# Laying the inputs of an attention, Fourier-mixing and feed-forward kernel out on the host

## The chip, the cores and the metric

The kernel runs on one core of a Trainium2 chip. The metric is the device time of one execution in microseconds. What the host does with the inputs before the launch, and with the output after it, is not part of that time.

## The reference

Eight batches of 576 tokens go through an attention of 8 heads of 64 channels, a Fourier mixing and a feed-forward layer. The attention has two parts that are added: a local one, in which a token sees the 7 tokens nearest to it, and a pooled one over means of 4 tokens.

```python
q_d = q.reshape(B, H, Sd, factor, D).mean(axis=3)           # factor 4, also k_d and v_d
out_d = sm_attn(q_d, k_d, v_d)
out_up = np.repeat(out_d, factor, axis=2)
mask = np.abs(pos[:, None] - pos[None, :]) < factor
scores = np.where(mask, scale * np.matmul(q, k.transpose(0, 1, 3, 2)), -1000000000.0)
x = out_up + softmax(scores) @ v                            # then (B, S, H * D)

mixed = np.real(np.fft.fft(np.fft.fft(x, axis=1), axis=2))
u = x + mixed
un = (u - mean(u)) / np.sqrt(var(u) + 1e-06)
out = u + np.maximum(un @ w_ch1, 0.0) @ w_ch2               # 512 -> 2048 -> 512
```

q, k and v are float32, the two weight matrices float64.

## The kernel before

**Phase 1** (the loop `while s < STEPS`, L836) makes the attention and the Fourier mixing. The local attention is cut into 40 units, five to a batch; a unit is a pair of windows of 64 tokens within a span of 128 tokens (`Unit`, L319). A step `s` of the loop loads unit s+3 (`load`), transposes unit s+2 (`transpose_in`), makes the scores of unit s+1 (`scores`), transposes the probabilities of unit s and multiplies unit s-1 by its values. The pooled attention of a batch (`Pooled`, L214) runs beside it, in parts of two heads, some two steps behind. Its last part leaves its result in the tile `odt` (L296); `store` (L302) writes that to a DRAM buffer `ud`, each row four times, and `add_up` (L482) has GpSimd's queue add those rows from DRAM onto the local attention's output `x0a`/`x0b` (then `x1a`.., `x2a`..) by an accumulating DMA. Then the folds for the Fourier transform begin with `xs` (`halves`, L500) on VectorE.

**What loads what.** Queries and keys come as rows: two DMAs a unit into `pairs`, in pieces of two tokens of one head, 512 B. ScalarE copies `pairs` to `qk` (L344), TensorE transposes that in eight steps into two PSUM banks `tk` (L351), ScalarE copies these to `qkT` in four (L357), and VectorE sums groups of four out of `qkT` (L376, `qdT`, `kdT`) for the pooled attention. The values of a unit come by two DMAs into `vaug`, in pieces of 256 B. For the pooled attention v comes once more, 64 DMAs with pieces of 1 KB, into `raw`, and GpSimd adds the four rows (L230, L231). Weights come as float64 in 64 quarters (`fetch`, L147), in pieces of 1 KB for `w1` and 2 KB for `w2`; VectorE, ScalarE and GpSimd turn each into float32 and split it into two parts (`to_f32`, `part_weights`). Five of the 64 are begun early in phase 1; most follow when phase 1 ends.

**Phase 2** is the feed-forward, 9 blocks of three to five tiles of 128 tokens (`Block`). A finished tile is stored by SyncE's queue where its tokens lie in order, else by an indirect DMA on GpSimd's queue (L808); the three tiles that are simplest to store are put last.

**What sets the order.** TensorE's program stands as the Python code issues it (`manual_schedule`, L821). On VectorE, ScalarE, GpSimd and SyncE's queue a scheduler puts the instructions in an order of its own, by a timeline that it works out when the kernel is built. Each engine then runs its list strictly in that order: an instruction that waits holds up all behind it. PSUM is a ring of eight banks in phase 1, and TensorE waits when the bank that it would write next has not been read.

## Time and profile before

| | us |
|---|---|
| median of 3 runs | 1357.9 |
| lowest and highest run | 1352.65, 1361.8 |
| span of the profiled execution | 1357.0 |
| TensorE busy | 1222.8 (90%) |
| VectorE busy | 635.3 (47%) |
| ScalarE busy | 376.4 (28%) |
| GpSimd busy | 422.5 (31%) |

The profile has one execution. Of its own time the page gives the span, from the first instruction to the last; the median of the runs is 0.9 us longer. In its rows PE is TensorE's matmuls, PEld its weight loads, DVE VectorE, ACT ScalarE, POOL GpSimd and SP SyncE. The DMA share is the mean busy share of the core's 16 DMA engines; it goes over 1 where packets overlap. The busy shares above are means over two phases that have little in common, so the time is best read by stretches.

### The profile page before, as it was taken

To read this page: it belongs to the slowest core of one execution; us is meant where nothing else is said; L and a number is where in the kernel's file an instruction comes from. 1 tells how busy PE (TensorE), PEld (TensorE's weight loads), DVE (VectorE), ACT (ScalarE), POOL (GpSimd) and SP (SyncE) were. 2 spreads that over 40 slices of the span, in tenths; PEclk is the share of its full clock that TensorE was granted. 3 is DMA by queue.
4 is the path that set the end of the run, shared out by engine and by line. 5 is a ranking of instruction groups with operands and counts; after the bars stand their busy time and mean duration, and the time that the engine had idled before them with its cause. 6 is when DMAs were issued, how large, how long until landed. Compare 5 with 4: busy or idle time off the path is not lost.

```text
span 1357.0 us, 21692 instructions
## 1 busy us (share of the span) xinstructions
PE 1222.8 (90%) x8556; PEld 1010.9 (74%) x8556; DVE 635.3 (47%) x1431; ACT 376.4 (28%) x878; POOL 422.5 (31%) x483
## 2 busy tenths in 40 slices
PE   5595986969779769988999999999999999999998
PEld 4484775857667657777888888888888888888897
DVE  3485695866966976888312213113123122131211
ACT  4483553645443222444111111111111111111111
POOL 3445465564634677887100101001000010010000
PEclk8887878979778769999999999999999999999999
DMA  9988748678456354342200101001001010010000
GB/s 180 234 176 186 162 122 168 161 146 182 120 129 143 90 132 123 101 125 86 70 1 8 55 0 62 1 0 62 1 0 63 0 55 8 1 55 0 1 31 24
DMA packets 133461, 110.76 MB, mean 82 GB/s; under 512 B 48262, under 2 KB 106920, under 8 KB 133104
## 3 DMA queue, kind: packets, MB, share of 16 engines
q1 hardware_dynamic: 125168, 89.38, 26.6%
q0 software_dynamic: 8192, 19.99, 6.8%
q8 instruction: 67, 1.10, 0.3%
q14 instruction: 34, 0.28, 0.1%
HBM read 81.06 MB, written 28.46 MB: 81 GB/s over the span
## 4 chain that ended last, share of the span: by engine, by line
PE 65%; DMA 14%; DVE 12%; POOL 4%; issue 4%; ACT 1%; SPq 1%; DVEq 0%; ACTq 0%; POOLq 0%
PE hps L780 26%; PE acc L798 9%; PE acc L796 9%; PE acc L797 9%; DMA ud<-odt 4%; DMA raw<-in_moe_w_ch_dram 3%; PE mix L576 3%; DMA x2b<-ud 2%; DVE wt L129 2%; DMA x0b<-ud 2%; DMA x1b<-ud 2%; PE sc L388 2%; PE av L442 1%; DVE wt L132 1%; PE tk L351 1%
## 5 line engine op out<-in xcount | busy, mean ns | idle before, releaser
L780 PE MATMUL hps<-unT,w1h 128*128 128x512 f32 (+2 forms) x1280 | 323.4, 375 | 14.1 <-DVE yl L551 8.9
L784 DVE SCALAR_TENSOR_TENSOR hl<-hps,hh 128x512 fp32r<-128x512 f32 (+2 forms) x160 | 101.5, 634 | 420.7 <-ACT hh L783 420.7
L780 PEld LDWEIGHTS hps<-unT,w1h 128*128 128x128 f32 x1280 | 234.2, 191 | 56.1 <-DVE yl L551 9.3
L783 ACT ACTIVATE hh<-hps 128x512 fp32r<-128x512 f32 (+2 forms) x160 | 88.5, 553 | 598.3 <-PE hps L780 592.4
L798 PE MATMUL acc<-w2h,hl 128*128 128x512 f32 x576 | 229.0, 398 | 7.2 <-DVE hl L784 7.0
L796 PE MATMUL acc<-w2h,hh 128*128 128x512 f32 x576 | 230.2, 400 | 4.3 <-ACT hh L783 4.3
L797 PE MATMUL acc<-w2l,hh 128*128 128x512 f32 x576 | 228.1, 396 | 0.0
L780 PE MATMUL hps<-unT,w1l 128*128 128x512 f32 (+2 forms) x640 | 160.6, 373 | 0.4 <-POOL w1l L169 0.4
L798 PEld LDWEIGHTS acc<-w2h,hl 128*128 128x128 f32 x576 | 108.7, 189 | 36.6 <-DVE hl L784 10.9
L780 PEld LDWEIGHTS hps<-unT,w1l 128*128 128x128 f32 x640 | 117.0, 191 | 19.8 <-POOL w1l L169 0.7
L796 PEld LDWEIGHTS acc<-w2h,hh 128*128 128x128 f32 x576 | 108.6, 188 | 28.8 <-ACT hh L783 5.8
L797 PEld LDWEIGHTS acc<-w2l,hh 128*128 128x128 f32 x576 | 108.7, 189 | 23.5
L808 POOL DMA_INDIRECT out_dram<-ut,rows x13 | 13.1, 1007 | 329.8 <-DVE ut L804 308.0
L230 POOL TENSOR_TENSOR raw<-raw 72x256 f32<-72x256 f32 x64 | 57.0, 898 | 94.1 <-DMA raw<-in_v_dram 92.1
L808 POOL DMA_INDIRECT out_dram<-x2a,rows x6 | 6.1, 1020 | 243.2 <-DVE x2a L804 148.1
L576 PE MATMUL mix<-chanm,yh 128*128 128x256 f32 (+1 forms) x192 | 47.0, 337 | 32.4 <-ACT sd L254 32.3
L388 PEld LDWEIGHTS sc<-qkT 64*64 64x64 f32 x1280 | 46.4, 151 | 21.4 <-issue 21.4
L442 PE MATMUL av<-vaug,pT 64*64 64x65 f32 x1280 | 51.9, 235 | 10.3 <-DVE yl L551 6.8
L576 PEld LDWEIGHTS mix<-chanm,yh 128*128 128x128 f32 (+1 forms) x192 | 31.2, 200 | 39.6 <-ACT sd L254 33.7
L351 PE MATMUL tk<-ident,qk 128*128 128x128 f32 x320 | 49.1, 301 | 10.6 <-DVE yl L551 6.5
L442 PEld LDWEIGHTS av<-vaug,pT 64*64 64x64 f32 x1280 | 45.7, 147 | 16.6 <-DVE yl L551 7.0
L254 ACT ACTIVATE sd<-sp,mxd 72x144 f32<-72x144 f32 x128 | 39.1, 377 | 64.2 <-DVE mxd L252 63.9
(161 smaller groups left out, 1847.0 us busy)
## 6 DMA issues: line engine op xcount, KB each, us to landing
raw<-in_moe_w_ch_dram SPq DMA_DIRECT2D x49, 256.0 KB
pairs<-in_k_dram SPq DMA_DIRECT2D x40, 256.0 KB
pairs<-in_q_dram SPq DMA_DIRECT2D x40, 256.0 KB
vaug<-in_v_dram SPq DMA_DIRECT2D x80, 128.0 KB
raw<-in_v_dram SPq DMA_DIRECT2D x64, 144.0 KB
ud<-odt SPq DMA_DIRECT2D x16, 576.0 KB
x2b<-in_moe_w_ch_dram SPq DMA_DIRECT2D x15, 256.0 KB
x2a<-um SPq DMA_DIRECT2D x15, 256.0 KB
```

The costliest lines, as they stand in the source:

```text
L230: nc.gpsimd.tensor_add(out=raw[:, :, half], in0=raw[:, :, half], in1=raw[:, :, 2 * D : 4 * D])
L254: nc.scalar.activation(out=sd[:, 2 * hl + t, :], in_=sp[:, t, :], func=AF.Exp, scale=2.0**-7, bias=mx[:, t : t + 1],)
L351: nc.tensor.transpose(tk[:, r, hp].rearrange("p i w -> p (i w)"), qk[:, r, 2 * (h0 + hp) : 2 * (h0 + hp) + 2, :].rearrange("p h d -> p (h ...
L388: nc.tensor.matmul(sc[r, a * W : (a + 1) * W], self.qkT[r, 0, a // 2, o : o + W], self.qkT[r, 1, a // 2, o : o + W], start=False, stop=Tru ...
L442: nc.tensor.matmul(av[r, a, :], pT[r, 4 * hh + a], va[r, 4 * hh + a, :], start=True, stop=True)
L576: nc.tensor.matmul(ps[:, par * HD : (par + 1) * HD], l, r, start=(i == 0), stop=(i == len(mms) - 1), skip_group_check=True,)
L780: nc.tensor.matmul(hps, a[:, c, :], unT[:, x, c, cols], start=(i == 0), stop=(i == len(mms) - 1))
L783: nc.scalar.activation(out=hh, in_=hps, func=AF.Relu)
L784: nc.vector.scalar_tensor_tensor(out=hl, in0=hps, scalar=0.0, in1=hh.bitcast(F32), op0=ALU.max, op1=ALU.subtract)
L796: nc.tensor.matmul(acc, hh[:, sl], w2h, start=(f == 0), stop=False)
L797: nc.tensor.matmul(acc, hh[:, sl], w2l, start=False, stop=False)
L798: nc.tensor.matmul(acc, hl[:, sl], w2h, start=False, stop=(f == NF - 1))
```

## The change

The host now lays out every input as the kernel reads it. `qk` holds, for each unit, queries and keys already transposed: one DMA of 128 rows of 4 KB straight into `qkT`. `vw` holds the values of a unit with the column of ones that `vaug` needs: one DMA of 128 rows of 2080 B. `vg` holds v for the pooled attention by groups of four rows, four heads at a time: 32 DMAs of 72 rows of 4 KB, and as many pairs of additions on GpSimd, each twice as wide. `wq` holds the quarters of the weights one behind the other, 128 rows of 2 KB each. Bytes loaded stay the same but for the column of ones.

On the chip `transpose_in` goes: 320 transposes on TensorE, 40 copies `qk` and 160 copies `qkT` on ScalarE, and the tiles `pairs` and `qk`. What is left of it, the sums of four, is called `sum_in`. `qkT` has four buffers in place of two, `raw` two in place of three, each twice as large. The rows of zeros that go to `ud` come from a tile of their own. In phase 2 all tiles are stored in their order by SyncE's queue, and the host puts the token rows in place at the end; the indirect stores go.

```diff
-NUM_V, NUM_PAIRS, NUM_QKT, NUM_P = 3, 3, 2, 2
-NUM_RAW, NUM_PT = 3, 4
+NUM_V, NUM_QKT, NUM_P = 3, 4, 2
+NUM_RAW, NUM_PT = 2, 4
...
         def load(self):
-            self.pairs = p2.tile([P, H, 2, D], F32, name="pairs", bufs=NUM_PAIRS)
-            for i, src in ((1, k), (0, q)):
-                nc.sync.dma_start(
-                    out=self.pairs[i * W : (i + 1) * W].rearrange("p h r d -> p h (r d)"),
-                    in_=src[self.b, :, self.s0 : self.s0 + P, :].rearrange("h (p r) d -> p h (r d)", r=2),
-                )
+            qkT = self.qkT = p2.tile([P, 2, HP, P], F32, name="qkT", bufs=NUM_QKT)
+            nc.sync.dma_start(out=qkT.rearrange("p i h w -> p (i h w)"), in_=qk[self.b, self.m])
 
         def load_v(self):
-            self.va = vaug[self.u % NUM_V]
-            for n2, (st, _) in enumerate(self.wins):
-                nc.sync.dma_start(
-                    out=self.va[n2 * W : (n2 + 1) * W, :, 0:D],
-                    in_=v[self.b, :, st : st + W, :].rearrange("h j d -> j h d"),
-                )
+            self.va = p2.tile([P, H, D + 1], F32, name="vaug", bufs=NUM_V)
+            nc.sync.dma_start(out=self.va.rearrange("p h d -> p (h d)"), in_=vw[self.b, self.m])
 
-        def transpose_in(self):
-            qk = p2.tile([P, 2, H, D], F32, name="qk", bufs=1)
-            nc.scalar.copy(out=qk.rearrange("p r h d -> p h r d"), in_=self.pairs)
-            qkT = self.qkT = p2.tile([P, 2, HP, P], F32, name="qkT", bufs=NUM_QKT)
-            for h0 in range(0, HP, 2):
...
+        def sum_in(self):
+            qkT = self.qkT
...
         def sum_v(self, i):
-            h0, t = 2 * (i // 2), i % 2
-            raw = pd.tile([GH, 2, 4 * D], F32, name="raw", bufs=NUM_RAW)
...
+            h0, t = 4 * (i // 2), i % 2
+            raw = pd.tile([GH, 4, 4 * D], F32, name="raw", bufs=NUM_RAW)
+            nc.sync.dma_start(out=raw.rearrange("g r c -> g (r c)"), in_=vg[self.b, i])
+            nc.gpsimd.tensor_add(out=raw[:, 0:2], in0=raw[:, 0:2], in1=raw[:, 2:4])
...
     def fetch(raw, tm, f, w, j):
+        src = wq[w - 1, f, j]
+        if wide:
+            nc.sync.dma_start(out=raw.bitcast(I32), in_=src.bitcast(I32))
...
         def finish(self, t):
             u, tt = uts[self.n % 2][t], self.order[t]
             nc.vector.tensor_add(out=u, in0=self.accs[t], in1=u)
-            if in_order(tt):
-                nc.sync.dma_start(out=out_rows[tt * P : (tt + 1) * P, :], in_=u)
-            else:
-                nc.gpsimd.indirect_dma_start(
...
+            nc.sync.dma_start(out=out_rows[tt * P : (tt + 1) * P, :], in_=u)
...
+    both = np.stack([q, k], axis=1).reshape(B, 2, HEADS // 2, 2, SEQ, DIM).transpose(0, 3, 5, 1, 2, 4)
+    spans = np.stack([both[..., s : s + P] for s in SPANS], axis=1)
+    data["qk"] = spans.reshape(B, NPAIR, P, -1)
...
-    return got[0]
+    return _tokens(got[0])
```

Since a scheduler orders four of the engines, the change also moves instructions that it does not name. First TensorE at the start of the program, behind its warm-up: `tk` are the transposes, `sc` the scores of a unit, `tpl` the transposes of its probabilities. Before:

```order
L351 MATMUL tk<-ident,qk 128x128 x16
L383 LDWEIGHTS identb
L383 MATMUL sc<-maskb,identb 128x512
L388 MATMUL sc<-qkT 64x64 x16
L351 MATMUL tk<-ident,qk 128x128 x8
```

and now:

```order
L341 LDWEIGHTS identb
L341 MATMUL sc<-maskb,identb 128x512
L346 MATMUL sc<-qkT 64x64 x16
L341 LDWEIGHTS identb
L341 MATMUL sc<-maskb,identb 128x512
```

The scores stand first, and wait for a load alone. Second VectorE in the fourth batch (number 3), the rows that end with `xs<-x0a,x0b`, the instruction that waits for the accumulating DMA of that batch; `odt` is the pooled result. Before, the last `odt` of batch 3 stands 27 rows ahead of `xs`, and the twelve rows up to `xs` are:

```order
L449 TENSOR_TENSOR x1b<-av,rs 128x256
L292 TENSOR_SCALAR rsd<-avd 72x4
L295 RECIPROCAL rsd<-rsd 72x4
L296 TENSOR_TENSOR odt<-avd,rsd 72x2x128
L551 TENSOR_TENSOR yl<-y,yh 128x320
L376 TENSOR_REDUCE qdT<-qkT 128x4x28
L376 TENSOR_REDUCE kdT<-qkT 128x4x28
L551 TENSOR_TENSOR yl<-y,yh 128x320
L398 TENSOR_REDUCE mx<-sc 128x8
L400 TENSOR_TENSOR sb<-sc,mx 128x512
L251 TENSOR_REDUCE mxd<-sp 72x2
L500 TENSOR_TENSOR xs<-x0a,x0b 128x1536
```

Now the last `odt` of batch 3 is the first of these rows:

```order
L282 TENSOR_TENSOR odt<-avd,rsd 72x2x128
L518 TENSOR_TENSOR yz<-yz 2x320
L356 TENSOR_REDUCE mx<-sc 128x8
L358 TENSOR_TENSOR sb<-sc,mx 128x512
L237 TENSOR_REDUCE mxd<-sp 72x2 x2
L238 TENSOR_SCALAR mxd<-mxd 72x2 x2
L509 TENSOR_TENSOR yl<-y,yh 128x320
L404 TENSOR_SCALAR rs<-av 128x4
L405 RECIPROCAL rs<-rs 128x4
L407 TENSOR_TENSOR x1b<-av,rs 128x256
L458 TENSOR_TENSOR xs<-x0a,x0b 128x1536
```

So fewer instructions stand between the last `odt` of a batch and its `xs` (the `odt` in the rows of before is already the first of the next batch). Third GpSimd where the large constants of the Fourier mixing are loaded (`seqm`, `chanm`). Before:

```order
L169 TENSOR_TENSOR w1l_77<-wt_81,w1h_76 128x256
L231 TENSOR_TENSOR vsum_109<-raw 72x2x64
L467 DMA seqm<-in_c_seq_dram 128x3840
L468 DMA chanm<-in_c_chan_dram 128x2048
L230 TENSOR_TENSOR raw<-raw 72x2x128 x3
```

and now:

```order
L214 TENSOR_TENSOR raw<-raw 72x512
L136 TENSOR_TENSOR wt_81<-raw_80,wt_81 128x256
L425 DMA seqm<-in_c_seq_dram 128x3840
L426 DMA chanm<-in_c_chan_dram 128x2048
L215 TENSOR_TENSOR vsum_106<-raw 72x4x64
```

The constants now follow directly on `wt<-raw,wt`, the last instruction that reads a weight quarter's place `raw_80`; the load of the next quarter waits for that same instruction.

124 lines of the change are left out of this document (47 added, 77 removed).

## The prediction

> **What bounds the kernel now.** I began with the busy time of each engine in stretches. I cut them where VectorE's timeline shows the end of a batch's last `odt` and the start of that batch's `xs`, because these two recur in every batch. One batch, in VectorE's timeline (start, duration, instruction, idle time before it):
>
> ```profile
> 203.78 0.42 DVE L296 TENSOR_TENSOR odt<-avd,rsd 72x256 f32<-72x256 f32 x1
> 228.32 5.02 DVE L500 TENSOR_TENSOR xs<-x2a,x2b 128x1536 f32<-128x1536 f32 x1 [8.66 <-DMA x2b<-ud]
> ```
>
> Batch 2's `odt` ends at 204.20 and its `xs` starts at 228.32. Between lie the store of `odt` to `ud` and the accumulating DMA. The other bounds were read likewise. Columns: stretch, length, busy time of PE, PEld, DVE, ACT and POOL, granted PE clock, DMA share, GB/s.
>
> ```profile
> span 1357.0 us, 21692 instructions
> ...
> 0.00:11.29 11.29, 5.63 (x20) 2.40 (x20) 2.24 (x6) 3.30 (x6) 6.34 (x15) 1.00 0.94 166
> 11.29:50.00 38.71, 26.52 (x383) 21.72 (x384) 20.76 (x56) 20.78 (x49) 18.19 (x33) 0.87 1.07 193
> 50.00:66.02 16.02, 5.47 (x89) 4.19 (x89) 3.56 (x8) 4.01 (x10) 3.34 (x6) 0.76 1.06 283
> 66.02:99.13 33.11, 30.86 (x503) 27.10 (x505) 29.56 (x98) 26.42 (x69) 15.66 (x29) 0.86 0.81 168
> 99.13:123.88 24.75, 18.84 (x262) 16.26 (x263) 9.76 (x31) 11.46 (x29) 9.32 (x14) 0.79 1.03 216
> ...
> 149.87:171.24 21.37, 16.83 (x207) 13.99 (x206) 7.97 (x23) 9.81 (x25) 6.79 (x9) 0.99 0.92 203
> ...
> 204.20:228.32 24.12, 20.06 (x263) 16.96 (x262) 10.31 (x28) 10.76 (x27) 8.60 (x13) 1.00 0.98 196
> 228.32:260.86 32.54, 25.96 (x333) 21.76 (x334) 31.45 (x76) 16.82 (x42) 23.22 (x23) 0.79 0.54 129
> 260.86:285.69 24.83, 19.92 (x262) 16.84 (x262) 10.21 (x28) 10.76 (x27) 8.69 (x12) 0.96 0.94 186
> 285.69:316.88 31.19, 25.18 (x333) 20.86 (x334) 30.83 (x76) 16.88 (x42) 23.84 (x23) 0.82 0.55 137
> 316.88:341.46 24.58, 19.95 (x262) 16.87 (x262) 10.21 (x29) 10.75 (x27) 8.66 (x13) 1.00 0.92 188
> ...
> 369.87:391.56 21.69, 16.73 (x233) 13.65 (x228) 9.94 (x29) 9.48 (x25) 6.60 (x6) 0.95 0.85 182
> ...
> 420.77:440.57 19.80, 16.89 (x193) 13.52 (x189) 8.68 (x32) 5.76 (x18) 7.93 (x9) 0.83 0.82 180
> ...
> 491.71:645.00 153.29, 134.37 (x706) 114.36 (x706) 130.74 (x242) 55.52 (x145) 123.15 (x130) 0.94 0.33 101
> 645.00:1357.00 712.00, 708.15 (x3174) 581.41 (x3171) 165.84 (x303) 91.22 (x159) 39.54 (x51) 1.00 0.07 24
> ```
>
> Four regimes stand here. From 645 on TensorE is busy 708 of 712 us at full clock: the feed-forward, of which the change touches only the stores. From 491.71 to 645 VectorE (131 of 153) and GpSimd (123) decode weights. From 99 to 491 every batch has two halves: a **chain half** of 20 to 25 us, in which VectorE works 8 to 10 us and then stands at `xs`, with the DMA engines 0.82 to 1.03 busy; and a **dense half**, in which VectorE is busy 31.45 of 32.54 us and TensorE 26. So a batch takes the latency of the chain and then the sum of VectorE's instructions behind `xs`. Up to 50 us the DMA engines are full at under 200 GB/s. VectorE's waits up to 99 us:
>
> ```profile
> DVE wt L129 <- DMA raw<-in_moe_w_ch_dram: 23.1, 4, 12.4
> DVE qdT L376 <- ACT qkT L357: 16.7, 7, 7.9
> ```
>
> They are 39.8 of its some 43 us without work there (99.13 less 2.24, 20.76, 3.56 and 29.56).
>
> **What goes, and is hidden.** The groups that leave, with their busy time and mean ns:
>
> ```profile
> L351 PE MATMUL tk<-ident,qk 128*128 128x128 f32 x320 | 49.1, 301 | 10.6 <-DVE yl L551 6.5 <-ACT qk L344 3.5 <-DVE sb L400 0.3
> L344 ACT COPY qk<-pairs 128x1024 f32<-128x1024 f32 x40 | 42.8, 1070 | 0.0
> L357 ACT COPY qkT<-tk 128x256 f32<-128x256 f32 x160 | 50.2, 399 | 18.8 <-PE tk L351 18.5
> ```
>
> That is 49 us of TensorE and 93 us of ScalarE, about 6 and 12 us a batch. I count them at nothing from 99 us on: in the dense half VectorE sets the pace, none of its steady work goes, and in the chain half all wait for DMAs. If this cover were gone, the 6 us a batch of TensorE would count, some 45 us over the rest of phase 1; that isn't to be had while VectorE is 97% busy.
>
> **The start, 0 to 99 us.** Less loading time, and two steps less before the first scores. What larger pieces do to the DMA engines is seen where such pieces move alone:
>
> ```profile
> 55.00:60.00 5.00, 0.68 (x5) 0.42 (x4) 0.00 (x0) 0.00 (x0) 0.52 (x1) 0.82 1.04 379
> 650.00:660.00 10.00, 10.00 (x45) 8.04 (x44) 6.08 (x14) 1.20 (x2) 3.31 (x4) 1.00 0.55 184
> ```
>
> The first is mostly the large constants: 379/1.04 = 364 GB/s with all engines busy. The second is rows of 2 KB: 184/0.55 = 335. Up to 50 us, with pieces of 256 B to 1 KB, it is 193/1.07 = 180. The loads of 2 to 4 KB therefore take about half the time (estimate from these three). Then: the first sums start when the first load lands, I take 5.5 us, in place of 11.29 (-6). The other 8.8 us of `qdT` waits become about 3, since ScalarE's copies and the slow loads go (-6). Of the 23.1 us of weight waits, 12.4 is one load beside the constants. The new order issues both at the same signal, so it may land ahead or wait again; I take 7 for it and 3 for the others (-13). Against it, new waits for loads and scores in the first steps (+2) and VectorE work that now stands ahead of batch 0's last `odt` (+2, counted from the order with the durations below). **Sum -21**, between -11 (the weight waits stay) and -30 (they all go).
>
> **The chain, batches 0 to 6.** In the last batches no queries, keys or values are loaded any more, and batch 6's chain takes 19.80 us. I take that as what store and accumulating DMA need alone. Over it lie 4.95, 1.57, 4.32, 5.03, 4.78 and 1.89 us in batches 0 to 5, together 22.5. The loads in the way now take half the time, so I take about half of it off: **-12**, between 0 and -22.
>
> **What the scheduler moved.** `xs` stands nearer to `odt` than before. Work that VectorE did while the chain ran is done behind it now, and the chain runs no faster for that. The durations (mean ns of one):
>
> ```profile
> L376 DVE TENSOR_REDUCE qdT<-qkT 128x112 f32<-128x448 f32 (+4 forms) x48 | 25.4, 542 | 22.4 <-ACT qkT L357 22.2
> L376 DVE TENSOR_REDUCE kdT<-qkT 128x112 f32<-128x448 f32 (+3 forms) x40 | 24.8, 621 | 0.0
> L398 DVE TENSOR_REDUCE mx<-sc 128x8 f32<-128x512 f32 x40 | 27.1, 678 | 1.5 <-PE sc L388 1.4
> L400 DVE TENSOR_TENSOR sb<-sc,mx 128x512 f32<-128x512 f32 x40 | 27.2, 679 | 0.2
> L251 DVE TENSOR_REDUCE mxd<-sp 72x2 f32<-72x288 f32 x64 | 27.2, 443 | 0.1
> L551 DVE TENSOR_TENSOR yl<-y,yh 128x320 fp32r<-128x320 f32 x32 | 15.4, 483 | 4.3 <-ACT yh L550 4.3
> L449 DVE TENSOR_TENSOR x1b<-av,rs 128x256 f32<-128x256 f32 (+1 forms) x18 | 7.6, 422 | 0.4
> L447 DVE RECIPROCAL rs<-rs 128x4 f32<-128x4 f32 x80 | 12.7, 169 | 1.1
> ```
>
> In batch 3 what no longer stands ahead of `xs` is three `qdT` and two `kdT` (1.6 + 1.2), one `mx`, one `sb` (1.4), one `mxd` (0.4), two `yl` (1.0), one `x1b` and one `odt` of like size (0.8), and four small ones at up to 0.17 (0.7): 7.1 us, and about 6.4 as they overlap by some 0.05 each. What remains ahead is about 3.8, against 10.21 in the row of 260.86. Counted in the same way, 4.5, 3.1, 9.4, 3.8, 9.4, 6.7 and 9.0 us remain in batches 0 to 6. The rows of before have 9.76, 7.97, 10.31, 10.21, 10.21, 9.94 and 8.68. That is 21 us longer dense halves, less the 2 us already counted at the start: **+19**. It counts in full only if the dense halves stay dense. Its other end is 10, if VectorE's small waits there for ScalarE go.
>
> **The rest.** VectorE's waits for weights behind 421 us:
>
> ```profile
> DVE wt L129 <- DMA raw<-in_moe_w_ch_dram: 7.0, 6, 3.0
> ```
>
> Half of the quarters come in pieces of 2 KB in place of 1 KB: **-2** (0 to -5). The stores that leave GpSimd's queue cost nothing: TensorE doesn't wait for them. SyncE's queue has fewer instructions; I count them at nothing, they are hidden by the chain.
>
> GpSimd's additions are half as many and twice as wide:
>
> ```profile
> L230 POOL TENSOR_TENSOR raw<-raw 72x256 f32<-72x256 f32 x64 | 57.0, 898 | 94.1 <-DMA raw<-in_v_dram 92.1
> ```
>
> So 57 us stay 57 us, and I take 0. A rule of the Trainium skill speaks against that (SBUF — State Buffer, section "SBUF: two separate sides"): VectorE and GpSimd share a port pair, and a VectorE instruction with two SBUF inputs waits until a GpSimd instruction that reads SBUF has ended. By it an addition of twice the length holds VectorE twice as long where they meet; with some ten such instructions in a dense half, a quarter of which meet one, for 0.4 us more each, my estimate by that page is +1 a batch, and the sum 1350. The `xs` of 5.02 us agrees with the lock, but no row of before has the wider addition.
>
> **The sum:** 1357.0 - 21 - 12 + 19 - 2 = 1341. The runs' median lies 0.9 above the span: 1342.
>
> **The rivals.**
>
> *The chain is cleared.* All chains come down to 19.8, the weights land ahead of the constants, the reordering costs 16: -30 - 22 + 16 - 2 = -38, so 1320. For it: the DMA engines are 0.9 and more busy in most chain halves, and the loads are what shrinks. Against it: batch 1 takes 21.4 us with all loads present, so they cannot cost 5 us each time.
>
> *The early `xs` decides: slower.* VectorE is held at `xs` while it still owes TensorE the scores' maxima and differences; TensorE stops earlier, resumes at the slow clock (0.79 to 0.82 in the dense halves), and then itself ends the dense half. In batches 0, 1, 3 and 5 TensorE loses about 5 us of work that it did beside the chain, 20 in all, of which some 5 go on top of VectorE's 19; the chain stays (0), and the start gives only the 6 of the first load and 4 more: -10 + 19 + 5 + 0 = +14, so 1372. It decides once chain and start together give less than 24. Against it: TensorE has 4 to 6 us a batch less to do.
>
> *Nothing remains.* The weight load waits behind the constants again and the chain gains a fifth: -14 - 4 + 19 - 2 = -1, so 1357. For it: the two are issued at the same signal.
>
> **How the numbers follow.** Forecast 0.48, chain cleared 0.20, nothing remains 0.20, slower 0.12. About 1% of the time, 13.6 us, is what a measurement of this kernel can tell from no change: under 1344 is faster, over 1371.5 slower. The forecast's own range is 1328 to 1356 from its terms' bounds; half of it and a little more (0.28) lies under 1344. Faster: 0.28 + 0.20 + a little of the third, 0.50; slower 0.11; same 0.39. The range reaches from 1316 to 1367: most of the cleared case is in, the slower one is out.
>
> **What would show it.** The first `qdT` at 5 to 6 us; batch 0's last `odt` ending near 78; chain halves of 21 to 23 us; dense halves some 5 us longer in batches 0, 1 and 3 (36 to 38 in batch 3), VectorE still 95% busy in them; the last stretch unchanged at 712. Chain halves still at 24 would make the forecast wrong upwards. Dense halves in which VectorE waits for TensorE would be the slower rival. A start over 88 us would mean that loads weren't what held it.

## The result and the profile after

The changed kernel takes 1393.73 us (median; 1391.41 to 1399.68) against 1356.95 us for the kernel before. The ratio is 1.026, with a 95% interval from 1.022 to 1.030. The forecast was 1342, so the direction was wrong, and the time lies above the range as well.

The profiled execution of the kernel after has a span of 1389.6 us and a mean TensorE clock of 0.896 (before: 1357.0 and 0.934). First its engines as a whole, and its DMA packets beside those of before:

```profile
PE 1214.0 (87%) x8236; PEld 998.6 (72%) x8236; DVE 636.9 (46%) x1428; ACT 292.3 (21%) x678; POOL 369.0 (27%) x388
DMA packets 50496, 110.84 MB, mean 80 GB/s; under 512 B 5494, under 2 KB 5784, under 8 KB 50144
```

```profile
DMA packets 133461, 110.76 MB, mean 82 GB/s; under 512 B 48262, under 2 KB 106920, under 8 KB 133104
```

The change did what it says. ScalarE's 84 us and GpSimd's 54 us are gone, and the same bytes come in 50496 packets in place of 133461. VectorE has as much work as before (636.9 against 635.3 us), and yet the span is 32.6 us longer. The stretches, cut at the same places as in the prediction (the columns too are the same), show where. Of the kernel after, the start, the chain and dense halves of batches 1 to 3 (with the first and the last chain half of the seven), and the two last stretches:

```profile
0.00:92.73 92.73, 66.57 (x897) 51.64 (x898) 62.18 (x171) 27.74 (x68) 40.25 (x58) 0.74 0.67 213
92.73:114.33 21.60, 8.11 (x145) 7.02 (x145) 5.24 (x16) 2.87 (x8) 6.63 (x6) 0.70 0.86 214
...
171.44:213.85 42.41, 33.69 (x406) 28.31 (x407) 36.02 (x95) 13.45 (x35) 20.71 (x18) 0.70 0.29 92
213.85:239.94 26.09, 19.66 (x269) 16.30 (x265) 10.57 (x27) 7.03 (x18) 7.63 (x9) 0.96 0.88 201
239.94:276.15 36.21, 23.32 (x270) 19.04 (x270) 31.96 (x77) 9.92 (x25) 20.62 (x18) 0.69 0.32 95
276.15:299.06 22.91, 14.61 (x176) 11.19 (x175) 4.04 (x11) 4.15 (x11) 7.50 (x8) 0.87 0.88 226
299.06:337.67 38.61, 31.59 (x390) 26.33 (x392) 36.14 (x92) 13.43 (x34) 20.26 (x18) 0.73 0.32 100
...
453.05:471.90 18.85, 16.45 (x170) 12.93 (x168) 8.60 (x32) 6.01 (x18) 8.03 (x9) 0.76 0.82 188
471.90:526.49 54.59, 38.87 (x195) 31.84 (x191) 39.69 (x93) 12.81 (x32) 31.64 (x29) 0.69 0.49 128
526.49:1389.60 863.11, 840.91 (x3867) 695.22 (x3867) 294.38 (x545) 146.49 (x304) 138.49 (x157) 0.99 0.11 37
```

The two last stretches of before, which the prediction did not cut in this way:

```profile
440.57:491.71 51.14, 34.55 (x162) 27.76 (x160) 41.36 (x91) 13.12 (x32) 34.40 (x29) 0.70 0.53 136
491.71:1357.00 865.29, 842.52 (x3877) 695.77 (x3876) 296.57 (x545) 146.74 (x304) 162.69 (x181) 0.99 0.12 37
```

Summed over all batches, with what the prediction had for each:

| stretch, us | before | after | difference | predicted |
|---|---|---|---|---|
| start, to batch 0's last `odt` | 99.13 | 92.73 | -6.4 | -21 |
| chain halves, batches 0 to 6 | 161.14 | 157.10 | -4.0 | -12 |
| dense halves, batches 0 to 5 | 180.30 | 222.07 | +41.8 | +19 (batch 6 too) |
| batch 6's dense half and batch 7's chain | 51.14 | 54.59 | +3.5 | |
| the rest | 865.29 | 863.11 | -2.2 | -2 |
| sum | 1357.0 | 1389.6 | +32.6 | -16 |

The loss is in the dense halves. In those of batches 0 to 5 VectorE was busy 174.19 of 180.30 us before, and is busy 192.35 of 222.07 us now. So 18.2 us more work stand there, which is the +19 of the prediction. But 23.6 us more stand there in which VectorE does nothing (29.7 against 6.1), and those the prediction did not have.

The loss follows the place of `xs`. What VectorE works in a chain half is what stands between the last `odt` and `xs`:

| batch | 0 | 1 | 2 | 3 | 4 | 5 |
|---|---|---|---|---|---|---|
| VectorE busy in the chain half before, us | 9.76 | 7.97 | 10.31 | 10.21 | 10.21 | 9.94 |
| after | 5.24 | 3.79 | 10.57 | 4.04 | 9.54 | 6.52 |
| dense half before, us | 25.99 | 32.96 | 32.54 | 31.19 | 28.41 | 29.21 |
| after | 35.87 | 42.41 | 36.21 | 38.61 | 30.49 | 38.49 |

So `xs` has come nearer in batches 0, 1, 3 and 5 alone, and not in every batch, as the section on the change has it from batch 3; and the dense halves of these four are 36.0 us longer, those of batches 2 and 4 only 5.8. Of the 29.7 us that VectorE stands in the six, 12.7 are at results of TensorE (1.0 before), 9.0 at the sums of four (2.5 before), and 3.9 at ScalarE's `yh` (none before). In the longest, batch 1's (171.44 to 213.85 us), its waits for TensorE and for a load include:

```profile
DVE xs L543 <- PE mix L534: 1.8, 1, 1.8
DVE mx L356 <- PE sc L346: 1.3, 1, 1.3
...
DVE kdT L334 <- DMA qkT<-in_qk_dram: 0.5, 1, 0.5
```

VectorE's waits up to 526.49 us in the kernel after (the line that waits, what it waited for, us in total, times, longest), and up to 491.71 us in the kernel before:

```profile
DVE kdT L334 <- DMA qkT<-in_qk_dram: 43.4, 17, 8.9
DVE xs L458 <- DMA x0b<-ud: 31.8, 3, 15.0
...
DVE wt L123 <- DMA raw<-in_wq_dram: 10.6, 5, 5.4
DVE mx L356 <- PE sc L346: 7.0, 10, 1.5
```

```profile
DVE wt L129 <- DMA raw<-in_moe_w_ch_dram: 26.4, 6, 12.4
DVE qdT L376 <- ACT qkT L357: 22.2, 16, 7.9
```

A new wait heads the list: VectorE stands 43.4 us at `kdT`, the sums of four out of `qkT`, until that unit's load has landed. Most of this total isn't where the loss is: 25.5 us lie in the start, which is 6.4 us shorter than before all the same, 8.9 in the chain half of batch 5, and 9.0 in the dense halves. The start's part (0 to 92.73 us):

```profile
DVE kdT L334 <- DMA qkT<-in_qk_dram: 25.5, 10, 5.8
```

But the wait shows an order that has changed. It is not a load that comes too late for its use. One case, which lies in the start, from the timeline of the kernel after (start, duration, instruction, idle time before it; unit 9's load on SyncE's queue, the scores of unit 6 on TensorE, then VectorE):

```profile
46.35 0.37 SPq L310 DMA_DIRECT2D qkT<-in_qk_dram  x1
49.84 1.97 PE L346 MATMUL sc<-qkT 64*64 64x64 f32 x32
52.17 0.42 DVE L407 TENSOR_TENSOR x0b<-av,rs 128x256 f32<-128x256 f32 x1
58.39 0.60 DVE L334 TENSOR_REDUCE kdT<-qkT 128x108 f32<-128x432 f32 x1 [5.80 <-DMA qkT<-in_qk_dram]
58.91 0.59 DVE L334 TENSOR_REDUCE qdT<-qkT 128x108 f32<-128x432 f32 x1
59.42 0.68 DVE L356 TENSOR_REDUCE mx<-sc 128x8 f32<-128x512 f32 x1
80.03 0.68 DVE L356 TENSOR_REDUCE mx<-sc 128x8 f32<-128x512 f32 x1
```

VectorE comes to unit 9's sum at 52.59 and stands there until 58.39. Behind it in VectorE's list is the maximum of unit 6 (`mx`), whose scores TensorE ended at 51.81. It runs at 59.42, 7.6 us after them. Unit 9's own maximum, which shows when that unit is really worked on, comes at 80.03. VectorE waits for data that its own step needs some 20 us later, and holds up what is due.

That sum did not stand there before. For each unit I counted by how many units the sum runs ahead of the maxima (its unit's number less the `mx` that VectorE has done by then), as a mean over units 3 to 39 of the trace:

| kernel | sums ahead of the maxima, units |
|---|---|
| before | 0.9 |
| after | 2.8 |

The scheduler puts an instruction where, by its own timeline, its input is there. Before, the input of a sum was made by eight transposes and four copies, and these came late enough that it stood beside its unit's scores. Now it is a load, and the sum moves up to where the scheduler believes that the load has landed. From unit 5 on the time from a sum to the maximum of the same unit is 38 us in the trace (mean; 12 before).

### The profile page after: what moved, and what is told of

Same layout as the page of the kernel before. It is cut to its first block, busy times and chain, and to the rows that moved or that the text cites. A ratio compares the mean times of both kernels' runs of the same rounds, so it can differ in the third digit from the quotient of the medians.

```text
span 1389.6 us, 20511 instructions
## 1 busy us (share of the span) xinstructions
PE 1214.0 (87%) x8236; PEld 998.6 (72%) x8236; DVE 636.9 (46%) x1428; ACT 292.3 (21%) x678; POOL 369.0 (27%) x388
## 2 busy tenths in 40 slices
DMA packets 50496, 110.84 MB, mean 80 GB/s; under 512 B 5494, under 2 KB 5784, under 8 KB 50144
## 4 chain that ended last, share of the span: by engine, by line
PE 64%; DMA 15%; DVE 11%; POOL 5%; issue 4%; ACT 1%; SPq 0%; DVEq 0%; POOLq 0%; ACTq 0%
PE hps L730 25%; PE acc L748 9%; PE acc L747 9%; PE acc L746 8%; DMA ud<-odt 4%; DMA qkT<-in_qk_dram 3%; DMA x1b<-ud 3%; PE mix L534 2%; PE y L507 2%; PE avd L270 2%; PE sc L346 2%; DMA x2b<-ud 2%; DMA x0b<-ud 2%; DVE wt L126 1%; DVE xeo L467 1%
## 5 line engine op out<-in xcount | busy, mean ns | idle before, releaser
L683 POOL TENSOR_TENSOR rstd<-rstd,mhalf 128x1 f32<-128x1 f32 x36 | 20.2, 607 | 555.2 <-DVE rstd L682 553.3
L400 PE MATMUL av<-vaug,pT 64*64 64x65 f32 x1280 | 57.9, 248 | 18.8 <-DVE odt L282 4.9
L270 PE MATMUL avd<-vsum,ptd 72*72 72x65 f32 x512 | 49.9, 263 | 25.2 <-ACT pT L383 17.6
L400 PEld LDWEIGHTS av<-vaug,pT 64*64 64x64 f32 x1280 | 50.5, 159 | 26.6 <-issue 13.5
L346 PEld LDWEIGHTS sc<-qkT 64*64 64x64 f32 x1280 | 51.4, 165 | 22.4 <-issue 21.5
L270 PEld LDWEIGHTS avd<-vsum,ptd 72*72 72x72 f32 x512 | 45.1, 176 | 28.5 <-ACT pT L383 17.8
L507 PE MATMUL y<-seqm,fh 128*128 128x320 f32 (+1 forms) x192 | 57.9, 389 | 2.0 <-DVE xm L543 1.5
L346 PE MATMUL sc<-qkT 64*64 64x64 f32 x1280 | 57.5, 254 | 0.0
```

The lines of the kernel that those rows point to most:

```text
L270: nc.tensor.matmul(av[:, t, hl, :], self.pts[h0][hl][:, kt, t * GH : (t + 1) * GH], self.vs[:, kt, h0 + hl, :], start=(kt == 0), stop=(kt ...
L346: nc.tensor.matmul(sc[r, a * W : (a + 1) * W], self.qkT[r, 0, a // 2, o : o + W], self.qkT[r, 1, a // 2, o : o + W], start=False, stop=Tru ...
L400: nc.tensor.matmul(av[r, a, :], pT[r, 4 * hh + a], va[r, 4 * hh + a, :], start=True, stop=True)
L507: nc.tensor.matmul(y, l, r, start=(i == 0), stop=(i == len(mms) - 1))
L683: nc.gpsimd.tensor_tensor(out=rstd, in0=rstd, in1=mhalf, op=ALU.pow)
```

## Experiments

All ratios below are against the kernel before, run on the same chip, with a 95% interval. The theories in question were these. *Place of `xs`*: VectorE stands at `xs` too early, with work left behind it (the prediction's rival). *Place of the sums*: VectorE stands at sums that aren't due. *Loads*: the loads of queries and keys come too late, whatever the order. *Clock*: TensorE, which has less to do, falls to the slow clock and becomes what is waited for. The expectations call these four A, F, B and D. C is that the loss lies in the other parts of the change, and E that the order made around a load counts, and not the load.

### Which part of the change costs

The first kernel is the one after with queries and keys as before: rows into `pairs`, copies, transposes, copies.

```diff
         def load(self):
...
-            qkT = self.qkT = p2.tile([P, 2, HP, P], F32, name="qkT", bufs=NUM_QKT)
-            nc.sync.dma_start(out=qkT.rearrange("p i h w -> p (i h w)"), in_=qk[self.b, self.m])
...
+            self.pairs = p2.tile([P, H, 2, D], F32, name="pairs", bufs=NUM_PAIRS)
...
         def sum_in(self):
-            qkT = self.qkT
...
+            qk = p2.tile([P, 2, H, D], F32, name="qk", bufs=1)
+            nc.scalar.copy(out=qk.rearrange("p r h d -> p h r d"), in_=self.pairs)
...
```

> The changed kernel with its queries and keys as before: loaded two tokens to a partition, turned on TensorE, copied on ScalarE; values, weights and the output order stay new. VectorE's xs then has 9 to 10 us of work ahead of it again in batches 0 to 5. Theory A (the early xs is the loss): the loss goes, and the gain of the other parts stays: 1345 to 1357 us. Theory B (VectorE stands at late loads of queries and keys): the loss goes too, 1345 to 1360. Theory C (the loss lies in the other parts: the zero rows put in front of the loads, fewer buffers for the grouped values, the wider additions): 1380 to 1394.

The second is the reverse, the kernel before with only queries and keys laid out anew.

> The kernel before with nothing changed but the queries and keys (laid out on the host, no transposes). Theories A and B: most of the loss is here, 1380 to 1395 us; A says that less of it is here in batch 3, where xs stays behind 9.8 us of work in this kernel (4.2 in the changed one), so that its dense half is 5 us shorter than the 38.6 of the changed one. Theory C: 1345 to 1360.

The next is the kernel before with only the values laid out anew (`vw`, `vg`, the rows of zeros), and then with only the weights and the order of the output rows.

> The kernel before with nothing changed but the values (both layouts, one load of a unit's windows with their ones, four sums in place of eight, the zero rows from one tile). xs has 9.3 us of work ahead in batches 2 to 5, 10.3 before. The run with old queries and keys was 17 us over the kernel before: if the values are it (loads issued earlier on SyncE's queue, which land beside the accumulating DMA; xs nearer by 1 us a batch): 1368 to 1376. If the weights are it: 1355 to 1362.

> The kernel before with nothing changed but the weights in the order of reading and the output order put right on the host. xs stands as before in all batches. By the prediction's terms 2 to 15 us less (1343 to 1356), if the weights' loads beside the constants become faster; if loads of the start only take turns: 1355 to 1360. If the 17 us of the run with old queries and keys come from here: 1368 to 1376.

| kernel | us | ratio | sums ahead | VectorE's wait at `kdT`/`qdT` |
|---|---|---|---|---|
| after without the new queries | 1374.42 | 1.011 (1.007 to 1.014) | 0.9 | 22.1 |
| only the new queries | 1387.64 | 1.021 (1.018 to 1.023) | 2.7 | 43.9 |
| only the new values | 1371.68 | 1.011 (1.005 to 1.016) | 0.9 | |
| only weights and output order | 1357.25 | 1.000 (0.997 to 1.002) | | |

Queries and keys alone cost 2.1%, values alone 1.1%, weights and output nothing. The first kernel's 1374.42 us lie in none of the ranges given for it: the loss is not all in one part. With the queries alone the sums are already 2.7 units ahead and the wait is already 43.9 us. In that kernel VectorE still works 9.95 and 9.93 us ahead of `xs` in batches 2 and 3 (10.57 and 4.04 in the kernel after), and its dense halves there are short:

```profile
242.58:273.72 31.14, 23.44 (x311) 18.90 (x312) 30.88 (x76) 9.79 (x24) 23.73 (x25) 0.75 0.50 134
297.67:331.39 33.72, 22.95 (x265) 18.48 (x265) 30.03 (x76) 9.27 (x23) 24.16 (x25) 0.70 0.40 106
```

That is 31.14 and 33.72 us where the kernel after has 36.21 and 38.61. In batch 3 the dense half is shorter where `xs` stands farther back, and VectorE has 6.1 us less work in it. In batch 2 `xs` stands as far back in both kernels, so its 5 us are something else: VectorE stands 4.25 us there in the kernel after, 2.8 of them at a sum, and 0.26 here. And since the sums are as early here as in the kernel after, early sums do not by themselves bring `xs` nearer.

The values remain a puzzle. In the kernel with the new values alone the chain halves sum to 165.9 us, against 161.14, and the dense halves to 188.9, against 180.30. In batch 3 the second unit's `pairs` are loaded 12.5 us after the last `odt`, where before it is 23.2. That more loads run beside the accumulating DMA could lengthen the chain, but batch 3's is 24.8 us in both, and no run shows it.

### The place of `xs`

Here `xs` of batch b may run only after the maxima of unit 5b+12 (5b+11 in batch 5), by a copy of one element that makes it depend on them, and the folds fall due 1.2 steps later.

```diff
+            if self.b < 6:
+                k = 5 * self.b + (12 if self.b < 5 else 11)
+                nc.vector.tensor_copy(out=xs[0:1, 0, 0:1], in_=units[k].mx[0:1, 0:1])
             nc.vector.tensor_add(out=xs, in0=xa, in1=xb)
```

> The changed kernel with xs held back in VectorE's order, behind the maxima of a later unit: 7.8 to 11.2 us of work stand between odt and xs in batches 0 to 5, in place of 3.5 to 9.7. Theory A: the dense halves lose the 17 us of work that was moved into them and some 10 of the waits that follow from it: 1362 to 1376 us. Theory B: the waits for the loads (43 us in the changed kernel) stay, 1385 to 1395.

It took 1374.46 us, 1.011 (1.009 to 1.014). But the next instruction on VectorE that hangs on a batch, the first reader of GpSimd's `xm`, had moved ahead of `xs`:

```profile
DVE xeo L473 <- POOL xm L463: 51.6, 3, 21.3
```

So that reader was held too, behind `xs`:

```diff
+            nc.vector.tensor_copy(out=xo[0:1, 0, 1:2], in_=xs[0:1, 0, 0:1])
             nc.vector.tensor_sub(out=xo[:, :, 1:HD], in0=xm[:, :, 1:HD], in1=xm[:, :, DM - 1 : HD : -1])
```

> As the run with xs held back, with the odd channels (the first VectorE instruction that reads xm) held behind xs too. There VectorE stood 51.6 us at that instruction, in three batches, so that the hold took only half. Theory A (the place of the first instruction that needs the chain): the dense halves, 220 us in that run and 249 in the changed kernel, come to 208 to 214, and the time to 1360 to 1370 us. If the place no longer counts: 1372 to 1378, as in that run.

This took 1370.15 us, 1.008 (1.006 to 1.011). The dense halves of batches 0 to 5 came down from 222.07 to 191.08 us, and VectorE's standing in them from 29.7 to 10.7, of which 2.0 are at results of TensorE (12.7 in the kernel after). So the place of `xs` is worth some 23 us of the 37 lost, and some 11 us against before remain, with the wait at `kdT` still 39.2 us (26.9 of them in the start, 5.0 in the dense halves).

### Earlier loads, more buffers, the rows of zeros

Queries and keys are loaded one unit earlier, with a fifth buffer:

```diff
-NUM_V, NUM_QKT, NUM_P = 3, 4, 2
+NUM_V, NUM_QKT, NUM_P = 3, 5, 2
...
-            lambda: (at(s + 3, "load"), at(s + 2, "sum_in")),
+            lambda: (at(s + 4, "load"), at(s + 2, "sum_in")),
...
+    units[3].load()
```

> The changed kernel with queries and keys loaded one step earlier into five buffers in place of four; the place of xs is as in the changed kernel (3.5 to 10.8 us of work ahead). Theory A: 1387 to 1396 us, the waits for the loads go and come back as the wait at xs. Theory B: VectorE's 43 us of waits for these loads fall to under 15 and the time by 20 or more, 1360 to 1373.

And the same together with both holds:

> Both holds and queries and keys loaded one step earlier into five buffers. If the two causes add up (19 or more for the place, 13 for the loads): 1345 to 1360 us, VectorE's waits at the sums under 25 us. If the earlier loads only move bytes into the chain: 1362 to 1372, with chain halves 1 to 2 us longer than in the run with both holds alone.

The wait at the sums with the early loads alone:

```profile
DVE kdT L334 <- DMA qkT<-in_qk_dram: 22.5, 11, 4.2
```

Alone it took 1380.54 us, 1.016 (1.014 to 1.018); with the holds 1370.74, 1.009 (1.007 to 1.011), the same as the holds alone. The wait halved, from 43.4 to 22.5 us. Alone this came with a gain of 1.0% on the kernel after: the dense halves fell to 201.6 us, but the chain halves grew from 157.10 to 164.1 us, and the start from 92.73 to 96.85. Together with the holds the chain halves grew from 159.6 to 163.3 us, the dense halves stayed, and nothing was gained.

Three more buffers for the values (`NUM_V = 6`), because SyncE's queue stands 117.6 us at the loads of `vaug`, with queries and keys behind them:

> The changed kernel with six buffers for the values of the local attention in place of three. SyncE's queue stood 117.6 us at their loads, with the queries and keys behind them; here it should stand there for under 20. Theory B (the queue's head holds the loads of queries and keys back): VectorE's waits at the sums fall from 43 us to under 25 and the time to 1372 to 1385 us. Theory A: 1388 to 1398; so too if the buffers of the queries and keys hold those loads.

The wait of SyncE's queue, in the kernel after and in this one:

```profile
SPq L314 <- PE av L400: 117.6, 22, 25.4
```

```profile
SPq L314 <- PE av L400: 104.9, 17, 27.7
```

It hardly changed, where under 20 us were expected, and the time was 1397.71 us, 1.028 (1.022 to 1.033): the same as the kernel after. The rows of zeros, which each batch now sets anew in its own tile as before:

```diff
-    zeros = pd.tile([8, DM], F32, name="zeros")
-    nc.gpsimd.memset(zeros, 0.0)
...
+        zeros = pd.tile([8, DM], F32, name="zeros", bufs=1)
+        nc.gpsimd.memset(zeros, 0.0)
```

> The changed kernel with the zero rows written again from a tile that each batch sets anew, so that their 16 DMA issues spread over the batches (in the changed kernel all stand at 6 to 24 us on SyncE's queue, ahead of the loads of the first batch). Theory C (these issues hold up the start): batch 0 ends its last odt 5 to 9 us earlier than 92.73 us, and the time is 1384 to 1389. If the start is held by the loads' own bytes: 92 to 94 us there, and 1391 to 1397.

1392.48 us, 1.025 (1.019 to 1.030): no difference either. Yet the wait at the sums fell in both, to 33.4 us with the buffers and 31.2 with the rows, from 43.4. In the start 12.0 and 5.4 us of waits for weights came in its place. So the total of this wait is not what it costs.

### TensorE's load, or the order?

To see whether TensorE's lost work matters, the transposes were put back as mere load: with both holds, each unit also transposes the identity eight times into two PSUM banks that nobody reads.

```diff
+            for _ in range(2):
+                tk = bank("tk")
+                for j in range(4):
+                    nc.tensor.transpose(tk[:, j * P : (j + 1) * P], ident, ident)
```

> Both holds, and eight transposes a unit that nobody reads put where those of the queries and keys stood on TensorE (this adds work and leaves none out). Theory D (without them TensorE has less to do, its clock is granted lower, 0.78 in the first 499 us with both holds against 0.84 before, and its results come later): the clock there rises to 0.82 or more, VectorE's dense halves fall from 218 us to some 208, the time is 1355 to 1364. If the clock doesn't matter: 1368 to 1378.

It took 1345.48 us, 0.989 (0.984 to 0.995), under both ranges: faster than before, with 320 idle transposes more than the kernel with both holds, which took 1370.15. The wait at `kdT` fell to 18.9 us. The clock theory seemed to have won. But an added instruction also makes the scheduler plan anew. So the next kernels tell load and order apart. Without the holds:

> The changed kernel without holds, with the eight transposes a unit that nobody reads. The scheduler then puts 10.6, 3.5, 7.0, 7.0, 7.0 and 8.9 us of work ahead of xs in batches 0 to 5 (4.6, 3.5, 9.7, 4.2, 9.7, 6.8 without). If the place of xs and the transposes add up (about 23 each): 1362 to 1372. If the transposes alone carry the gain: 1345 to 1355. If only both together do: 1378 to 1390.

1363.88 us, 1.004 (1.002 to 1.006), with 30.0 us at `kdT`. Holds and load, and the values as before:

> Both holds and the fillers, with the values loaded and summed as before (two pieces a unit, eight sums a batch, zero rows spread). Alone, the new values cost 15 us. If that cost stands beside the others: 1328 to 1338. If the fillers' order has taken it away: 1342 to 1350.

1351.56 us, 0.994 (0.992 to 0.996). This is no faster than with the new values, so the 1.1% that these cost alone isn't a price that stands beside the others. It lies over both ranges. VectorE stands 36.9 us at the sums in this kernel (43.4 in the kernel after), and yet it is faster than the kernel before.

A first try at the order alone kept the order of the kernel with the load, and made the load small, products of four columns in place of transposes; another kernel was ordered around these products and had full transposes put in.

> The order of the run with fillers, to the instruction, on VectorE, ScalarE, GpSimd and SyncE, but the eight transposes a unit cut down to products of 4 columns, so that TensorE's load is that of the changed kernel. Theory D (the load keeps TensorE's clock up and its results early): the time goes back to 1362 to 1372 and the clock of the whole run to 0.91 to 0.92. Theory E (not the load but the order that the scheduler makes around the transposes): 1336 to 1350.

> The other way round: the order that the scheduler makes around products of 4 columns (near that of the run with both holds), held fast, and the full transposes put in their places. Theory D: 1345 to 1356, clock 0.93 or more. Theory E: 1368 to 1385, the load only adds to TensorE.

The first took 1376.68 us, 1.011 (1.006 to 1.015), but it is a spoiled control. The "small" products in it, and the transposes in the kernel before it:

```profile
L325 PE MATMUL tk<-ident 128*128 128x4 f32 x640 | 91.2, 275 | 1.0 <-DVE sb L367 1.0
```

```profile
L321 PE MATMUL tk<-ident 128*128 128x128 f32 x320 | 49.4, 302 | 1.5 <-DVE x0b L412 1.4
```

320 products of four columns show as 640 records and took 91.2 us, the 320 transposes 49.4. So the load had been made larger, not smaller, and VectorE waited 47.5 us at `mx` for scores (7.0 in the kernel after). The second took 1397.33 us, 1.026 (1.023 to 1.030), in an order that is neither of the two in question.

The clean pair followed. Call order A the one that the scheduler made with both holds and no load, order B the one that it made with the load. Each was now held to the instruction on VectorE, ScalarE, GpSimd and SyncE's queue by dependencies that only order and make nothing wait: order B with no load at all, and order A with the whole load.

> Four cases: the order that the scheduler makes with the fillers (B) or without (A), held fast on VectorE, ScalarE, GpSimd and SyncE, and the fillers on TensorE or not. A without is 1370 us, B with is 1345. This one is B without a single filler (the products of 4 columns in the earlier try took 91 us of TensorE, more than the transposes' 49). Theory E (the order): 1338 to 1350. Theory D (TensorE's load and clock): 1365 to 1378, VectorE's waits at the sums of four near 39 us as in A without.

> A with the fillers: the order of the run with both holds, to the instruction, and eight unread transposes a unit on TensorE. Theory E: 1368 to 1390 (the fillers only add work). Theory D: 1343 to 1355. If both orders come near 1358, load and order each carry half.

| | no load | with 320 transposes |
|---|---|---|
| order A | 1370.15, 1.008 (1.006 to 1.011) | 1371.21, 1.011 (1.006 to 1.016) |
| order B | 1350.9, 0.996 (0.993 to 0.998) | 1345.48, 0.989 (0.984 to 0.995) |

The 1350.9 us lie just over theory E's range and far under D's. Down a column the order alone changes, and the ratio falls by 0.013 without the load and by 0.022 with it. Along a row only the load changes: the ratio moves by 0.003 in order A, within its interval, and by 0.006 in order B, where the intervals overlap. Order A without the load, then with it, up to the same place in the program, with the clock in the column before the DMA share:

```profile
core 0: 1364.9 us, clock 0.914
0.00:498.82 498.82, 375.08 (x4369) 303.03 (x4369) 347.23 (x897) 146.26 (x374) 236.80 (x232) 0.78 0.58 157
```

```profile
core 0: 1371.1 us, clock 0.935
0.00:507.21 507.21, 385.12 (x4689) 316.23 (x4689) 351.46 (x898) 146.37 (x374) 239.60 (x233) 0.85 0.57 155
```

The load does raise the granted clock, from 0.78 to 0.85 in phase 1, and the stretch isn't shorter for it. So for these two orders the clock theory falls, and the order decides. Both hold `xs` back; whether the clock counts where `xs` stands early, no run tells apart from the order. What differs between the orders shows at the sums, in order A without load, A with load and B without:

```profile
DVE kdT L335 <- DMA qkT<-in_qk_dram: 39.2, 16, 7.2
```

```profile
DVE kdT L341 <- DMA qkT<-in_qk_dram: 38.9, 18, 7.5
```

```profile
DVE kdT L341 <- DMA qkT<-in_qk_dram: 16.5, 12, 3.8
```

In order B the sums are as far ahead as in A (2.8 units), but its loads land in time more often. So sums that stand early need not cost much. Which part of order B makes it faster is not shown: its start (80.97 against 94.04 us) and its dense halves (178.4 against 191.08) are shorter than order A's, its chain halves longer (166.4 against 159.6).

### The sums put back

If the early sums cost, it must help to put them where they were. This kernel is the one after, with no load and no added instruction. `behind` only orders: the sums of unit u stand behind the `sb` (scores less maxima) of unit u-2, so one unit ahead as before, and `xs` and the first reader of `xm` are held at the places of order A, with the folds 1.2 steps later as there.

```diff
+                if self.u >= 2:
+                    behind(added, units[self.u - 2].subtracted)
...
+            if self.b < 6:
+                behind(self.summed, units[5 * self.b + (12 if self.b < 5 else 11)].subtracted)
...
+            behind(odd, self.summed)
...
-            lambda: (at(s + 3, "load"), at(s + 2, "sum_in")),
-            lambda: at(s + 1, "scores"),
+            lambda: at(s + 3, "load"),
+            lambda: (at(s + 1, "scores"), at(s + 2, "sum_in")),
```

> The changed kernel, no fillers, with two orders laid down for VectorE and no instruction added: xs and the first reader of xm behind the same places as in the run with both holds (6.9 to 10.6 us of work ahead of xs in batches 0 to 5), and the sums of four of a unit behind the sb of two units before it, so that they stand one unit ahead of their scores as before the change (three ahead in the changed kernel and in both orders A and B). The run with both holds alone took 1370 us. Theory F (the sums standing two units too early make VectorE wait for loads that it doesn't need yet): waits at the sums under 8 us (39 with the holds alone), batch 0's last odt at 80 to 88 us, 1333 to 1350 us. If only the order of the loads and stores that B has counts, and not the place of the sums: 1362 to 1372.

It took 1343.47 us, 0.990 (0.987 to 0.993). By the ratios that is 3.5% under the kernel after, 1.8% under the one with `xs` and its reader alone held, and 1.0% under the kernel before. The sums are 1.0 unit ahead. The waits at the sums, and at the weights in the start (0 to 89.85 us):

```profile
DVE kdT L340 <- DMA qkT<-in_qk_dram: 6.5, 2, 3.5
```

```profile
DVE wt L124 <- DMA raw<-in_wq_dram: 18.6, 4, 7.9
```

In the start of order A without load these were 26.9 and 0.4 us. So of 20.4 us that are gone at the sums, 18.2 came back at the weights, and the start is 4.2 us shorter; its 89.85 us miss the 80 to 88 that were expected.

Its start, two batches of its chain and dense halves, and its last two stretches:

```profile
0.00:89.85 89.85, 65.47 (x906) 50.24 (x907) 59.70 (x167) 28.43 (x68) 40.06 (x58) 0.79 0.70 222
...
142.16:163.92 21.76, 17.90 (x237) 14.90 (x237) 8.86 (x24) 6.17 (x16) 6.56 (x6) 0.99 0.82 203
163.92:195.57 31.65, 22.82 (x318) 18.84 (x318) 27.98 (x79) 11.20 (x28) 22.35 (x19) 0.79 0.42 123
...
251.58:274.94 23.36, 18.49 (x242) 15.38 (x241) 10.08 (x28) 6.72 (x19) 6.51 (x6) 0.95 0.82 209
274.94:307.24 32.30, 24.78 (x314) 19.75 (x314) 32.18 (x75) 10.44 (x26) 24.21 (x19) 0.77 0.43 125
...
424.73:473.95 49.22, 41.55 (x223) 34.03 (x220) 43.49 (x94) 13.41 (x32) 31.00 (x29) 0.72 0.57 143
473.95:1336.10 862.15, 839.40 (x3857) 691.56 (x3856) 295.14 (x542) 146.97 (x305) 137.37 (x157) 0.99 0.12 38
```

VectorE again works about 10 us in a chain half (10.08 in the one at 251.58), where the kernel after has 4.04 in batch 3, and it is busy 32.18 of 32.30 us in the dense half behind it. Summed as above:

| stretch, us | before | after | `xs` and its reader held (order A) | sums put back too |
|---|---|---|---|---|
| start | 99.13 | 92.73 | 94.04 | 89.85 |
| chain halves, batches 0 to 6 | 161.14 | 157.10 | 159.59 | 152.51 |
| dense halves, batches 0 to 5 | 180.30 | 222.07 | 191.08 | 182.37 |
| of these, VectorE busy | 174.19 | 192.35 | 180.40 | 174.90 |
| batch 6's dense half and batch 7's chain | 51.14 | 54.59 | 54.11 | 49.22 |
| the rest | 865.29 | 863.11 | 866.07 | 862.15 |

The profiled execution of the last kernel is its fastest, 5.6 us under the median (order A's 3.5), so the table shows where, and the ratio shows how much.

One reserve: the scheduler makes its whole plan anew whenever one place is fixed, so this kernel differs from the one with `xs` held in more than the sums, above all in when the loads are issued. What it gains on order A is spread over all stretches, while the wait at the sums was mostly in the start. Order B shows that such differences can be worth as much by themselves. So it is shown that the order alone, with the layout unchanged, moves the ratio from 1.026 to 0.990; that the second half of this comes from the place of the sums itself is likely and not shown.

## Why the prediction was wrong

**What goes, and is hidden** (nothing for 49 us of TensorE and 93 us of ScalarE): right. The work of TensorE was put back in order A, and the time was 1371.21 us against 1370.15. ScalarE's copies were not put back by themselves.

**The start** (-21): mis-sized, it measured -6.4. The first sum came at 4.77 us, near the forecast of 5.5, and the weight waits went from 23.1 to 0.8 us, further than forecast. But "The other 8.8 us of `qdT` waits become about 3" was wrong. VectorE stands 25.5 us for `qkT` in the start (16.7 before), at sums that have moved ahead, and 6.05 us of work (62.18 against 56.13) stand there that stood later, where I had counted 2. "A start over 88 us would mean that loads weren't what held it": at 92.73 it was the order that held it. Order B without load reaches batch 0's last `odt` at 80.97 us with the same layout, near the 78 of the forecast.

**The chain** (-12): -4.0, and -8.6 with the sums put back. The step rested on loads that take half the time. In the chain halves the rate hardly rose: 188 to 226 GB/s over the seven, against 180 to 216 before.

**What the scheduler moved** (+19): this is the step that failed. It measured +41.8 in batches 0 to 5 and +3.5 behind them. What it counts is right: VectorE has 18.2 us more work in the dense halves. But it prices nothing except this work, under the condition that "the dense halves stay dense", and gives the term a lower end of 10 and no upper one. Even with every term at its upper bound the sum ends at 1366, and with every one at its lower bound at 1311, which is wider than the 1328 to 1356 given and still leaves the result out. They did not stay dense: 23.6 us more of standing came on top of the work. VectorE, which was to set the pace there, waits for results of TensorE (11.7 us more than before), at the sums of four for loads that aren't due yet (6.5 more) and for ScalarE (3.9). With `xs` and its reader held back the standing falls from 29.7 to 10.7 us, that at TensorE from 12.7 to 2.0, and the dense halves from 222.07 to 191.08. So an `xs` that stands early costs more than the work that it puts off.

The step also missed that the same order moves the sums of four from one unit ahead of the maxima to three. With them at their old distance as well, VectorE is again busy 174.90 of 182.37 us, and the time is 1343.47 us, 1.8% less than with `xs` alone held. How much of this is VectorE's standing at the sums stays open: with more buffers and with the rows of zeros that wait fell and the time did not, and with the values as before the time fell and the wait hardly did.

That 1343.47 us lie next to the forecast of 1342 is luck. In that kernel the start gains 9.3 us and not 21, the chain 8.6 and not 12, and the dense halves lose 2.1 and not 19.

**The rest** (-2): -2.2.

**GpSimd's additions** (0): right. They come half as often and take longer each, but less than twice:

```profile
L214 POOL TENSOR_TENSOR raw<-raw 72x512 f32<-72x512 f32 x32 | 44.2, 1382 | 45.3 <-DMA raw<-in_vg_dram 44.6 <-PE tp L254 0.6
```

So 57.0 us of additions became 44.2, and VectorE's busy time stayed at 636.9 against 635.3 us over the whole kernel. The result of 1350 that the prediction worked out beside its sum from the Trainium skill (SBUF — State Buffer, section "SBUF: two separate sides") is not borne out in the balance: 1.6 us more are seen, not 8. Whether single instructions were held is not told apart by these runs.

**The rivals.** "The early `xs` decides" had the direction and more of the mechanism than the forecast: it named batches 0, 1, 3 and 5, where 36.0 of the 41.8 us lie, and VectorE that then waits for TensorE, whose sign ("Dense halves in which VectorE waits for TensorE") is seen with 12.7 us. It was too small, with 5 us on top of VectorE's work where 23.6 were measured, and it did not have the sums. Its slow clock is open. The granted clock in the dense halves is lower than before, 0.61 to 0.78 against 0.67 to 0.82, but whether that makes TensorE late there, no run shows. The Trainium skill (TensorE: Matmul & The Clock Gate, section "What's actually happening") has the clock follow how busy TensorE has been of late. The trace agrees: with the 320 transposes the granted clock in phase 1 is 0.85 in place of 0.78. In order A the faster clock saved nothing (1371.21 us against 1370.15): `xs` is held there, and without the load VectorE stands only 2.0 us for TensorE in the dense halves. "The chain is cleared" and "Nothing remains" both took the old order on VectorE for granted, as the forecast did.

**What stays open.** Why the values alone cost 1.1%, and why they cost nothing beside the holds and the load. What in order B brings its loads in time. What the early sums cost by themselves, and what the new plan gives that comes with putting them back. Why the start, with the sums put back, takes 89.85 us and not the 78 forecast; 18.6 us of waits for weights are back in it.

## What to carry to other kernels

When a change takes a stage away in front of an instruction, ask not only what the stage cost but also what held that instruction in its place: in a program that a scheduler orders, a freed instruction moves up to where the scheduler believes its input ready, and on an engine that works in order a wait there holds all that is due. Compare, for every instruction that lost a producer, how far it stands ahead of its use before and after. Price an early place by what then falls due behind it, and not by the total of its wait: of the 43.4 us at the sums, 25.5 lay in a start that was shorter than before. And when added or removed load on an engine changes the time, hold the order fixed before giving the cause to the load or to the clock.

## What the runs showed of the hardware

A plain float32 product of only four columns isn't cheap: 128x4 products took 275 ns a record at two records each, against 302 ns and one record for a 128x128 transpose. TensorE's rows in that kernel's first 97.90 us show busy 92.92 us at a granted clock of only 0.76:

```profile
0.00:97.90 97.90, 92.92 (x1096) 80.30 (x1096) 57.72 (x170) 28.14 (x68) 40.65 (x58) 0.76 0.67 204
```

So an engine that the profile shows as nearly always busy need not be at the full clock: the feed-forward of the kernel before, busy 708.15 of 712.00 us, has a clock of 1.00. The busy time of the profile does not by itself tell the clock.

Larger DMA pieces freed the DMA engines more than they raised the rate. Packets are mostly of 2 to 4 KB in place of 256 B to 1 KB, and 50496 in place of 133461. The start of before, to set beside that of after (213 GB/s at a share of 0.67):

```profile
0.00:99.13 99.13, 68.48 (x994) 55.41 (x996) 56.13 (x166) 54.50 (x132) 43.54 (x81) 0.86 0.97 196
```

So 196 GB/s took a share of 0.97, and 213 now take 0.67. In the chain halves, beside the accumulating DMA, the rate went only from 180 to 216 GB/s to 188 to 226, at a share of 0.82 to 0.91 (0.82 to 1.03 before).
